# The last product of VectorE's exponentials on GpSimd, narrower products of P, and three smaller edits

## The chip, the core and the metric

The kernel runs on one core of a Trainium2 chip. The core has five engines with queues of their own that wait for one another through semaphores: TensorE (PE in the profile; its weight loads are PEld), VectorE (DVE), ScalarE (ACT), GpSimd (POOL) and SyncE (SP), which here only issues transfers. The metric is the time of one execution on the device. The kernel before takes 808.6 us, the median of three runs (807.6 to 808.67).

## The reference

Two attention blocks read the same input `x` (2048 rows of 512), and a gate per row mixes their results:

```
g = sigmoid(sum(x * gate_w))                       # one number per row
A: q, k, v = x @ wqkv_A   (32 heads of 16)
   P = softmax(q k^T / 4);  a = (P v) @ wo_A       # 32 x 2048 x 2048 exponentials
B: q, k, v = x @ wqkv_B
   phi(t) = where(t > 0, t + 1, exp(t)) + 1e-6
   b = (phi(q) (phi(k)^T v) / (phi(q) sum phi(k))) @ wo_B
out = g * a + (1 - g) * b
```

The work lies in A: a score and an exponential for each head, query and key, and the product of the exponentials with v. B is linear in the rows and small.

## The kernel before

**Units and rounds.** A unit is 128 keys by 512 queries of one head. A round is four heads and 512 queries, that is 64 units; there are 32 rounds and 2048 units. The score matmul of a unit uses 32 of TensorE's 128 rows, and three such matmuls of different heads run side by side. They write three PSUM banks: banks 0 to 2 and 3 to 5 are two slots that take turns (`SLOTS`). ScalarE then makes the exponentials of a whole slot with one instruction (L1540), 1536 columns wide into the buffer `PT`.

**The second source of exponentials.** For some units VectorE makes the exponential. The unit is claimed in one of two ways. It takes the third bank of a slot, so that ScalarE's instruction is only 1024 wide (`claim_in_group`), or it takes the spare bank (`claim_beside`, `misc_step`). VectorE copies the score from PSUM into `YI` as a clamped 16-bit integer (L1186). Three claimed units make a triple of 1536 columns, and `close_tri` queues five instructions for it, all from SBUF to SBUF in `DP`: g from the bits of y (L1200), h from the low bits of y (L1202), w = h * h (L1204), e from the high bits of g (L1205), and w = w * g (L1207). The exponential is a weighted sum of e, g and w; the weights are in two scaled copies of v, `V2`. So a unit from VectorE enters TensorE as three stationary operands where one from ScalarE enters as one.

**Products of P.** `pv_fns` multiplies 128 queries of a unit (stationary) with v (moving). A moving operand is 64 columns: 32 of `Vaug` (16 of v, a column of ones for the row sum, zeros) and 32 columns of zeros beside them. All products of a round gather in one bank, `acc_bank`; after 64 units `round_end` divides by the row sum, multiplies with the gate and sends the result by a transposing transfer to `OT`.

**Everything else** runs between these: the projections for A's next 128 columns of q, k and v, all of B, the gate (`step_gate`), and the output matmuls. Each such step takes one spare bank (`MISC`, bank 7), in pieces of two to sixteen matmuls, where `misc_step` finds room.

**What sets the order.** The program is laid out in advance by a planner in the kernel's Python code. It keeps an estimated clock for each engine (`PE.t`, `AC.t`, `DV.t`), with constants for each kind of work: `QK_T`, `PV_T` (four products of P), `d_sb` and `d_psum` for VectorE, `LAT` for a wait. The main loop (to L1575) issues a slot's scores, then ScalarE's instruction. Until the next slot is free by that clock it fills TensorE with products of P, steps and claims. `pump` hands queued VectorE work out by priority; the triples have the lowest. On the chip the engines follow the order so made, each in its own queue; a semaphore wait that the planner took to be short can be long. `mac_share` adds up how much of TensorE's array the last 3 us used, and where it is under `MAC_LOW` (0.5), `fill` adds a matmul of zeros (`warm`). GpSimd has only the preparations of the first 13 us.

**The start.** The first slots are woven with the transposes and projections that they need (`stage`, `run_now`), each in a bank from `rot_bank`, which from the first slot on has bank 7 alone. **The end.** Four output blocks are left: two are copied by ScalarE (L1616), two get their first part added by VectorE (L1621), all into `outl`, which lies in the `g` part of `DP`. Each of the four names all of `r_G` as written, so each waits for the one before.

## Time and profile before

| | |
|---|---|
| median of three runs | 808.6 us |
| the profiled execution: time, span | 809.02 us, 807.3 us |
| ScalarE busy | 788.0 us (98% of the span); L1540 x649 |
| TensorE busy | 768.8 us (95%); products of P x10976 |
| VectorE busy | 734.9 us (91%); 348 units, 116 triples |
| GpSimd busy | 11.5 us (1%) |
| first and last L1540 | starts at 9.0 us, ends at 799.1 us |

Busy time counts a stretch once even when two instructions of an engine overlap in it. On ScalarE and VectorE the next instruction starts before the one before has ended, so what an instruction costs its engine is the time from its start to the next start, shorter than its own duration. TensorE's ends are modelled, so there too start to start is the measure. The row of granted clock says what part of TensorE's full clock was granted.

### The profile page before, as it was taken

How to read it: one execution, taken by the hardware profiler on the slowest of the kernel's cores; microseconds unless marked ns; L12 is line 12 of the kernel's file. 1: busy time of each engine (PE TensorE's matmuls, PEld its weight loads, DVE VectorE, ACT ScalarE, POOL GpSimd, SP SyncE). 2: the span in 40 equal slices, each digit the busy share in tenths (PEclk: the TensorE clock that was granted, in tenths of full speed). 3: DMA queues.
4: the chain of work that ended last, by engine and by line, in shares of the span. 5: the costliest groups of instructions: out<-in, count | busy, mean ns of one | idle time of the engine just before them, and what ended most of it. 6: DMA issues, size and time to landing. Idle time of an engine off the chain costs nothing.

```text
span 807.3 us, 31603 instructions
## 1 busy us (share of the span) xinstructions
PE 768.8 (95%) x14060; PEld 478.4 (59%) x14060; DVE 734.9 (91%) x1253; ACT 788.0 (98%) x689; POOL 11.5 (1%) x21
## 2 busy tenths in 40 slices
PE   7999999999999999999999999999999999999997
PEld 3655655655565666555556566556665556565664
DVE  4689999798999999998999999999999998999983
ACT  5899999999999999999999999999999999999996
POOL 5000000000000000000000000000000000000000
PEclk9889999999999999999999999999999999999999
DMA  9200000000000001000000100101111001000100
GB/s 252 86 9 15 2 2 16 2 14 4 2 15 3 15 4 9 9 2 15 2 16 9 22 16 9 28 9 16 29 22 29 9 19 25 10 22 15 22 3 30
DMA packets 32492, 16.96 MB, mean 21 GB/s; under 512 B 24608, under 2 KB 31200, under 8 KB 32352
## 3 DMA queue, kind: packets, MB, share of 16 engines
q1 hardware_dynamic: 30336, 13.32, 7.0%
q8 instruction: 112, 1.84, 0.9%
q10 hardware_dynamic: 2016, 1.57, 0.8%
q14 instruction: 28, 0.23, 0.1%
HBM read 5.90 MB, written 2.10 MB: 10 GB/s over the span
## 4 chain that ended last, share of the span: by engine, by line
PE 40%; ACT 39%; issue 14%; DVE 7%; ACTq 0%; POOL 0%; DVEq 0%; POOLq 0%
PE ps L525 39%; ACT PT L1540 38%; DVE YI L1186 1%; ACT epool L791 1%; DVE DP L1204 1%; DVE DP L1207 1%; DVE DP L1200 0%; PE ps L528 0%; DVE xT L1457 0%; DVE DP L1205 0%; DVE DP L1202 0%; DVE phi L796 0%; DVE Vaug L745 0%; DVE Osb L1049 0%; DVE KT L690 0%
## 5 line engine op out<-in xcount | busy, mean ns | idle before, releaser
L1540 ACT ACTIVATE PT<-ps 128x1536 bf16<-128x1536 f32 (+1 forms) x649 | 780.6, 1558 | 6.8 <-PE ps L525 6.6
L525 PE MATMUL ps<-Qpad,KT 32*128 32x512 bf16 x2048 | 272.9, 387 | 25.3 <-ACT PT L1540 15.7
L525 PEld LDWEIGHTS ps<-Vaug,PT 128*128 128x128 bf16 x6800 | 230.1, 98 | 110.9 <-issue 105.9
L525 PE MATMUL ps<-Vaug,PT 128*128 128x64 bf16 x6800 | 287.9, 195 | 0.3 <-DVE Osb L1049 0.2
L1186 DVE TENSOR_SCALAR YI<-ps 128x512 int16<-128x512 f32 x348 | 239.3, 688 | 23.4 <-PE ps L525 13.2
L525 PE MATMUL ps<-Vaug,DP 128*128 128x64 bf16 x4176 | 163.1, 194 | 1.2 <-DVE Osb L1049 1.2
L525 PEld LDWEIGHTS ps<-Vaug,DP 128*128 128x128 bf16 x4176 | 138.4, 98 | 25.5 <-issue 18.2
L525 PEld LDWEIGHTS ps<-Qpad,KT 32*128 32x128 bf16 x2048 | 69.0, 91 | 138.8 <-ACT PT L1540 106.0
L1204 DVE TENSOR_TENSOR DP<-DP 128x1536 bf16<-128x1536 uint16 x116 | 110.8, 955 | 2.5
L1207 DVE TENSOR_TENSOR DP<-DP 128x1536 bf16<-128x1536 bf16 x116 | 110.3, 951 | 0.0
L1200 DVE TENSOR_SCALAR DP<-YI 128x1536 uint16<-128x1536 uint16 x116 | 64.3, 554 | 0.9
L1202 DVE TENSOR_SCALAR DP<-YI 128x1536 uint16<-128x1536 uint16 x116 | 64.2, 553 | 0.0
L1205 DVE TENSOR_SCALAR DP<-DP 128x1536 uint16<-128x1536 uint16 x116 | 63.9, 551 | 0.0
L525 PE MATMUL ps<-wB,xT 128*128 128x512 bf16 x128 | 37.6, 382 | 1.3 <-DVE phi L796 1.1
L525 PE MATMUL ps<-xT,wA 128*128 128x512 bf16 x108 | 31.9, 391 | 0.0
L791 ACT ACTIVATE epool<-ps 128x512 bf16<-128x512 f32 x32 | 27.7, 866 | 0.0
L796 DVE SCALAR_TENSOR_TENSOR phi<-ps,epool 128x512 bf16<-128x512 f32 x32 | 22.0, 688 | 1.6
L525 PE MATMUL ps<-xT,wB 128*128 128x512 bf16 x64 | 18.3, 381 | 0.0
L525 PE MATMUL ps<-woA,OT 128*128 128x512 bf16 x64 | 18.0, 381 | 0.0
L745 DVE CAST Vaug<-ps 128x512 bf16<-128x512 f32 x16 | 11.0, 689 | 7.6 <-PE ps L525 7.3
L525 PE MATMUL ps<-woB,OBT 128*128 128x512 bf16 x64 | 17.5, 381 | 0.1
L1047 DVE RECIPROCAL rraw<-ps 128x16 f32<-128x16 f32 x32 | 8.1, 253 | 9.1 <-PE ps L525 9.0
(85 smaller groups left out, 244.4 us busy)
## 6 DMA issues: line engine op xcount, KB each, us to landing
Qpad<-Qs SPq DMA_DIRECT2D x124, 16.0 KB, 1.8
wA<-in_A_wqkv_dram SPq DMA_DIRECT2D x1, 1536.0 KB, 7.0
wB<-in_B_wqkv_dram SPq DMA_DIRECT2D x1, 1536.0 KB, 10.6
out_dram<-outt SPq DMA_DIRECT2D x12, 128.0 KB, 1.7
phi<-in_A_x_dram ACTq DMA_DIRECT2D x3, 256.0 KB, 6.1
PT<-in_A_x_dram ACTq DMA_DIRECT2D x1, 512.0 KB, 3.9
woA<-in_A_wo_dram SPq DMA_DIRECT2D x1, 512.0 KB, 12.1
woB<-in_B_wo_dram SPq DMA_DIRECT2D x1, 512.0 KB, 11.9
```

Of the source, the lines that this page charges most:

```text
L525: return lambda: nc.tensor.matmul(o, lhsT=l, rhs=r, start=start, stop=stop, skip_group_check=sg)
L745: ops = [(lambda: nc.vector.tensor_copy(Vaug[:, par, 4 * v:4 * v + 4, :, 0:16], src), [r_bank[b]], [r_V[par][v]], d_psum(512), lambda: v_d ...
L791: op(AC, lambda: nc.scalar.activation(epool[:, s, :], bank_ap(b), ACT.Exp), reads=[r_bank[b]], writes=[r_e[s]], dur=0.6, issue=0.48)
L796: (lambda: nc.vector.scalar_tensor_tensor(out=dst, in0=bank_ap(b), scalar=0.0, in1=epool[:, s, :], op0=ALU.max, op1=ALU.add), [r_bank[b], ...
L1047: (lambda: nc.vector.reciprocal(raw, acc4[:, :, :, 16]), [r_acc], [r_rraw], 0.26, None),
L1186: push(0 if in_group else 1, [(lambda: nc.vector.tensor_scalar(YI[:, yi, 512 * k:512 * (k + 1)], bank_ap(b), Y_LO, Y_HI, op0=ALU.max, op1= ...
L1200: (lambda: nc.vector.tensor_scalar(gb, y, 0x8000, 3, op0=ALU.bitwise_xor, op1=ALU.logical_shift_right), [r_YI[yi]], [r_G[dp]], d_sb(n, 0.2 ...
L1202: (lambda: nc.vector.tensor_scalar(hh, y, 0x3FF, 0x400, op0=ALU.bitwise_and, op1=ALU.bitwise_or), [r_YI[yi]], [r_DP[dp]], d_sb(n, 0.25), N ...
L1204: (lambda: nc.vector.tensor_tensor(w, hh, hh, ALU.mult), [r_DP[dp]], [r_DP[dp]], d_sb(n, 0.5), None),
L1205: (lambda: nc.vector.tensor_single_scalar(eb, gb, 0xFF80, ALU.bitwise_and), [r_G[dp]], [r_E[dp]], d_sb(n, 0.25), None),
L1207: (lambda: nc.vector.tensor_tensor(w, w, g, ALU.mult), [r_DP[dp], r_G[dp]], [r_DP[dp]], d_sb(n, 0.5), None)])
L1540: op(AC, lambda slot=slot, b0=b0, n=n: nc.scalar.activation(PT[:, slot, 0:n], ps[:, 512 * b0:512 * b0 + n], ACT.Exp, scale=LN2 / FRAC, bia ...
```

## The change

- **Last product.** `w = w * g` leaves VectorE's queue and is issued on GpSimd as soon as the planner has issued `w = h * h`. Products of P from `DP` now wait for GpSimd. The planner takes `0.3 us + n * 2.2 ns` for it, that is 3.68 us for 1536.
- **52 columns.** The moving operand of a product of P is 26 columns of v and 26 of zeros in place of 32 and 32. The planner's `PV_T` goes from 0.117 to 0.1012.
- **Gate.** Its matmuls come in 16 pieces of four in place of four of sixteen, and a piece is put off while `mac_share` is under 0.4.
- **Start.** Until the first product of P, `rot_bank` also uses the accumulator's bank; the first v projection goes behind the fourth slot in place of the first.
- **End.** The four output copies no longer name `r_G`.
- **Planner's numbers.** `PT_URGENT`, `PV_LAG`, `LATE`, `MIN_LEFT`, `CLAIM_LOAD` and `GPR` are set anew, so the whole order differs. The plan that comes out has 393 units and 131 triples on VectorE and 361 + 286 instructions L1540 of 1536 and 1024 columns, where before it had 348 units, 116 triples and 403 + 245 (and one of 512). The matmuls of zeros go from 27 to 45 (13 of them in the start in both).

```diff
-PV_T = 0.117
+PVW = 26
+PV_T = 0.1012
+PV_MAC = 0.087
+POOL_FIX, POOL_T = 0.3, 2.2e-3
...
+        GATE_N = 1
+        GATE_MAC = .4
...
-                for t in range(NQC):
+                for t in range(0, NTB, GATE_N):
                     fns = []
-                    for tb in range(4 * t, 4 * t + 4):
+                    for tb in range(t, t + GATE_N):
...
-                    out_.append((fns, rd, 0.6, 0.01))
+                    out_.append((fns, rd, 0.15 * GATE_N, 0.0025 * GATE_N))
...
-                if c + 64 <= 512:
-                    mv = bass.AP(tensor=v0.tensor, offset=own, ap=[list(v0.ap[0]), [zero_off - own, 2], [1, 32]])
-                    o = acc[:, c:c + 64]
+                if c + 2 * PVW <= 512:
+                    mv = bass.AP(tensor=v0.tensor, offset=own, ap=[list(v0.ap[0]), [zero_off - own, 2], [1, PVW]])
+                    o = acc[:, c:c + 2 * PVW]
...
-        PT_URGENT = 15
+        PT_URGENT = 13
...
-                     dur=PV_T * n, mac=0.107 * n)
+                     dur=PV_T * n, mac=PV_MAC * n)
...
-        MIN_LEFT, MIN_LEFT_LAST = 30, 24
+        MIN_LEFT, MIN_LEFT_LAST = 24, 24
...
+            def last_product():
+                op(PO, lambda: nc.gpsimd.tensor_tensor(w, w, g, ALU.mult), reads=[r_DP[dp], r_G[dp]], writes=[r_DP[dp]],
+                   dur=POOL_FIX + n * POOL_T)
...
-                (lambda: nc.vector.tensor_tensor(w, hh, hh, ALU.mult), [r_DP[dp]], [r_DP[dp]], d_sb(n, 0.5), None),
+                (lambda: nc.vector.tensor_tensor(w, hh, hh, ALU.mult), [r_DP[dp]], [r_DP[dp]], d_sb(n, 0.5), last_product),
                 (lambda: nc.vector.tensor_single_scalar(eb, gb, 0xFF80, ALU.bitwise_and),
-                 [r_G[dp]], [r_E[dp]], d_sb(n, 0.25), None),
-                (lambda: nc.vector.tensor_tensor(w, w, g, ALU.mult), [r_DP[dp], r_G[dp]], [r_DP[dp]], d_sb(n, 0.5), None)])
+                 [r_G[dp]], [r_E[dp]], d_sb(n, 0.25), None)])
...
-        GPR = 16.9
+        GPR = 16.6
...
+                if hold[0][2][0][3] < 0.01 and mac_share(now) < GATE_MAC:
+                    return False
...
-        CLAIM_LOAD = 4.0
+        CLAIM_LOAD = 5.0
...
-        PV_LAG = 15
-        LATE = 12
+        PV_LAG = 13
+        LATE = 14
...
-        V0_AT = 1
+        V0_AT = 4
...
-            b = misc_banks[bank_turn[0] % len(misc_banks)]
+            banks = misc_banks + [acc_bank[0]] if acc_n[0] == 0 and acc_round[0] == 0 else misc_banks
+            b = banks[bank_turn[0] % len(banks)]
...
-            op(AC, lambda k=k, o=o: nc.scalar.copy(outl[:, k, :], o), reads=[r_bank[free[k]]], writes=[r_outl[k]] + r_G, dur=0.6)
+            op(AC, lambda k=k, o=o: nc.scalar.copy(outl[:, k, :], o), reads=[r_bank[free[k]]], writes=[r_outl[k]], dur=0.6)
...
-               reads=[r_bank[free[k]], r_pre[k]], writes=[r_outl[k]] + r_G, dur=d_psum(512))
+               reads=[r_bank[free[k]], r_pre[k]], writes=[r_outl[k]], dur=d_psum(512))
```

More of the change, by code (lines that the diff above doesn't have):

```diff
@@ L1012, in pv_fns @@
                 c = 128 * qb + 32 * j
-                if c + 64 <= 512:
-                    mv = bass.AP(tensor=v0.tensor, offset=own, ap=[list(v0.ap[0]), [zero_off - own, 2], [1, 32]])
-                    o = acc[:, c:c + 64]
-                else:
-                    mv = bass.AP(tensor=v0.tensor, offset=zero_off, ap=[list(v0.ap[0]), [own - zero_off, 2], [1, 32]])
-                    o = acc[:, c - 32:c + 32]
+                if c + 2 * PVW <= 512:
+                    mv = bass.AP(tensor=v0.tensor, offset=own, ap=[list(v0.ap[0]), [zero_off - own, 2], [1, PVW]])
+                    o = acc[:, c:c + 2 * PVW]
+                else:
+                    mv = bass.AP(tensor=v0.tensor, offset=zero_off, ap=[list(v0.ap[0]), [own - zero_off, 2], [1, PVW]])
+                    o = acc[:, c - PVW:c + PVW]
                 fns.append(f_mm(o, p_ap[:, 128 * qb:128 * (qb + 1)], mv, start=(first and qb == 0), stop=False, sg=True))
```

## The prediction

> **What bounds the kernel now.** First the page's busy times, then the stretches by stage: from 65 to 760 us ScalarE is hardly ever idle, while TensorE and VectorE are each idle a few per cent.

> ```profile
> PE 768.8 (95%) x14060; PEld 478.4 (59%) x14060; DVE 734.9 (91%) x1253; ACT 788.0 (98%) x689; POOL 11.5 (1%) x21
> ...
> PE 40%; ACT 39%; issue 14%; DVE 7%; ACTq 0%; POOL 0%; DVEq 0%; POOLq 0%
> ```
> ```profile
> 30.00:35.00 5.00, 4.98 (x131) 3.75 (x126) 4.72 (x9) 4.33 (x5) 0.00 (x0) 1.00 0.02 3
> 35.00:45.30 10.30, 9.94 (x109) 5.39 (x109) 7.54 (x15) 7.97 (x9) 0.00 (x0) 0.50 0.01 2
> ...
> 200.00:400.00 200.00, 192.90 (x3600) 120.53 (x3596) 189.67 (x327) 200.00 (x181) 0.00 (x0) 1.00 0.04 8
> ```

> Columns: stretch, length, busy time of PE, PEld, DVE, ACT, POOL, granted clock, DMA share, GB/s. ScalarE sets the pace, and from 35 to 45.3 us TensorE ran at half clock and left ScalarE idle for 2.3 us. What an exponential costs ScalarE is read start to start:

> ```profile
> L1540 ACT ACTIVATE PT<-ps 128x1536 bf16<-128x1536 f32 x403 | 592.0, 1715 | 3.7 <-PE ps L525 3.6
> L1540 ACT ACTIVATE PT<-ps 128x1024 bf16<-128x1024 f32 x245 | 272.6, 1301 | 3.1 <-PE ps L525 3.0
> ```

> From start to start, with nothing to wait for, the trace has 1.330 us behind a 1536 and 0.903 behind a 1024, though each itself lasts longer; behind an epool (B's exponential) it is 0.477. The sum 403 x 1.330 + 245 x 0.903 + 0.5 + 32 x 0.477 + 0.1 is 773.1 us of the 790.1 from the first L1540 (9.0) to the end of the last (799.1). So only 17 us are lost there: 2.9 before 20 us, 5.0 from 20 to 60, and about 0.24 per 20 us after. Faster means fewer ScalarE columns, if TensorE and VectorE can carry what ScalarE drops.

> **The change, part by part.**

> *ScalarE.* The changed program's order has 361 of 1536 and 286 of 1024, no 512, and the same 32 epool. Its sum is 361 x 1.330 + 286 x 0.903 + 15.3 + 0.1 = 753.8: **19.3 us less**. The 41 more short ones cost something, because behind a 1024 TensorE has less time to refill the slot: the mean start-to-start loss is 0.05 us behind a 1024 and 0.02 behind a 1536, so 41 x 0.05 = **+2**.

> *VectorE.* From start to start the trace gives: L1186 0.60, L1200, L1202 and L1205 0.47 (0.57 where the next waits for it), L1204 and L1207 0.87 each:

> ```profile
> 302.13 0.55 DVE L1205 TENSOR_SCALAR DP<-DP 128x1536 uint16<-128x1536 uint16 x1
> 302.60 0.95 DVE L1207 TENSOR_TENSOR DP<-DP 128x1536 bf16<-128x1536 bf16 x1
> 303.47 0.56 DVE L1200 TENSOR_SCALAR DP<-YI 128x1536 uint16<-128x1536 uint16 x1
> ```

> Removed: 116 x 0.87 = 101 us. Added: 15 triples of 3 x 0.60 + 0.47 + 0.57 + 0.87 + 0.47 = 4.18, 63 us. All VectorE work start to start is 714 before, so 676 after: 86% of a shorter span where it was 88%. It hides under ScalarE as before, if nothing slows it.

> *GpSimd.* 131 products of 1536 columns, two inputs and one output, all in SBUF. No row shows one. Nearest rows: filling 8192 columns took 6.92 us (0.84 ns a column, one write); a select (one read, one write) took 0.19 us at 8 columns and 0.29 and 0.34 at 128, so 0.8 to 1.2 ns a column over a fixed 0.19. If a second read adds one such pass, the product is 0.2 + 1536 x (1.7 to 2.4 ns) = 2.8 to 3.9 us; I take 3.3, the middle. [...] 131 x 3.3 is 432 us of 785, so GpSimd is not the bound; the planner counts 3.68, so up to there products of P from `DP` come no earlier than their data. At 3.9 TensorE would wait up to 0.2 us per triple, 29 us if all were bare; nearly all of it can hide while TensorE has slack. Cost taken: 0, bounds 0 and 29.

> *TensorE.* A 64-column product of P, and what a narrow matmul costs at least:

> ```profile
> 28.88 0.52 PE L525 MATMUL ps<-Vaug,PT 128*128 128x64 bf16 x12
> 29.66 1.57 PE L525 MATMUL ps<-Vaug,PT 128*128 128x64 bf16 x48
> ...
> 32.27 0.55 PE L525 MATMUL ps<-gw,xT 128*128 128x1 bf16 x16
> 33.07 0.95 PE L525 MATMUL ps<-gw,xT 128*128 128x1 bf16 x32
> ```

> (1.57 - 0.52) / 36 = 29 ns for 64 columns; (0.95 - 0.55) / 16 = 25 ns for one column. 52 columns lie between: by proportion 24, so the 25 binds. 10976 x 29 = 318 us become 11336 x 25 = 283, while 18 more matmuls of zeros at 0.217 add 4: TensorE gets 31 us lighter. It is not the bound, so this buys no time itself; it keeps TensorE from becoming the bound when ScalarE quickens. Were 52 columns as dear as 64, TensorE would instead grow by 10 + 4 us while the span shrinks by 24; its busy share would pass ScalarE's in places (a rival).

> *Clock.* The gate's 64 one-column matmuls stand at 32.3 to 34.0 and 38.9 us; in the 3.4 us from 32 the array's use was 0.22, and at 35.05 the granted clock halved, for 10.2 us. In steady state the use falls to 0.39 at the least and the clock stays whole. Between 35 and 46 us ScalarE lost 3.1 us. The changed order puts at most 12 gate matmuls together, with products of P between. **-3.1**; bounds -3.1, and +3 for one such stretch elsewhere, since narrower products lower the use (mean 0.66) by some 0.05.

> *Start.* The losses up to 35 us other than the clock's are 2.9 plus 1.7 (0.52 at 21, 0.35 at 27, 0.78 at 30); the largest, 1.4 at 13.7, is TensorE waiting for VectorE's copies out of the one spare bank. A second bank overlaps these, but a later first v heaps up products of P, as in the x48 run above. Bounds -4.6 and +1.5; I take the middle, **-1.5**.

> *End.*

> ```profile
> 801.86 0.58 ACT L1616 CAST DP<-ps 128x512 bf16<-128x512 f32 x1 [2.71 <-PE ps L525]
> ...
> 802.89 0.58 ACT L1616 CAST DP<-ps 128x512 bf16<-128x512 f32 x1 [0.45 <-PE ps L525]
> ```
> ```profile
> 803.58 0.69 DVE L1621 TENSOR_TENSOR DP<-ps,phi 128x512 bf16<-128x512 f32 x1 [2.07 <-ACT DP L1616]
> ...
> 804.38 0.68 DVE L1621 TENSOR_TENSOR DP<-ps,phi 128x512 bf16<-128x512 f32 x1
> ```

> VectorE waited 2.07 us for ScalarE's copy only through `r_G`. Its block is TensorE's second of four, so its first add can start near 802.1 and the second end near 803.6 in place of 805.06. Then ScalarE's own second store (issued at 803.51) is next to last. **-1.4**; bounds 0 and -1.6.

> Sum against the profiled execution: 809.02 - 19.3 + 2 - 3.1 - 1.5 - 1.4 = **785.7**, taken as 786. That execution is 0.4 above the median; both stand within what a measurement of this kernel tells from no change, 0.2% or 1.6 us.

> **The rivals.**

> *1. GpSimd's product shuts VectorE out.* L1200, L1202, L1205 (0.30 ns a column) and L1204 (two SBUF operands) go through SBUF alone; the other 1.8 us of a triple, L1186, comes from PSUM. If GpSimd's product and such an instruction exclude each other for their whole length, VectorE stands still whenever one comes up too early. In the changed order, between a product and the next such instruction (L1205 let past) there is PSUM work of 1.34 us on average, and none at 28 of 131. The sum of what is missing to 3.3 us is 260 us. VectorE's 676 becomes 936, plus some 20 at the ends: **956 us**; 896 at 2.8 us, 1032 at 3.9. The chain: claimed units stay in their banks, TensorE's scores wait for these, ScalarE for the scores. It decides once the mean stall passes 786 - 20 - 676 = 90 us over 131, 0.7 us a product. The trace is nearly silent: GpSimd's last instruction ends at 12.7 us and the first triple comes some 20 us later. Beside GpSimd's 6.92 us fill, three VectorE fills of 256 columns in SBUF started at once and took 0.27 us each: both can be in SBUF together, at least where neither reads and VectorE goes at 0.83 ns a column. [...] Chance 0.20: the only side-by-side rows speak against an exclusion of every kind, but none has a quick instruction.

> *2. They only slow each other.* GpSimd is busy 3.3 of 5.9 us per triple; of the 2.37 us of SBUF work 1.3 falls beside it. A slowing by half to double costs 0.65 to 1.3 us a triple, 85 to 170 us against 90 of slack: **786 to 866**, middle 815. Chance 0.09.

> *3. TensorE eats the gain:* the product comes later than 3.68, or 52 columns cost 29 ns. Of 29 to 45 us (33 + 12) of added TensorE time about a third shows, since its idle share is some 8%: **797**. For it: the planner's order fixes every wait beforehand. Against: the one-column row. Chance 0.09.

> **How the numbers follow.** The forecast, 776 to 796 around **786**, gets 0.62: losses along the way by bounds of +-5, start and clock together +-5. Rivals 1 to 3 have 0.20, 0.09, 0.09. Faster by over 0.2%: 0.62 + 0.08 of rival 3 = 0.70; within: 0.03 (edge of 2 and 3); slower: 0.20 + the rest, 0.27. The range leaves rival 1 out whole: **775 to 820**.

> **What would show it.** Right: start-to-start 1.33 and 0.90 on ScalarE unchanged, its busy share still 98%, products of P at 25 ns, no row of half clock at 35 us, GpSimd near 3.3 us each, L1621 without a wait for ScalarE. Wrong by rival 1: L1200, L1202 or L1204 with idle time released by GpSimd or with durations of several us, and L1540 waiting for scores. By rival 2: the same rows at 0.7 to 1 us in place of 0.55. By rival 3: weight loads of `Vaug,DP` waiting for GpSimd.

## The result and the profile after

The changed kernel takes 1038.4 us (median; 1034.5 to 1039.0) where the kernel before, beside it, takes 808.6: a ratio of 1.283, 95% interval 1.280 to 1.286. The forecast of 786 us and its range of 775 to 820 were wrong; the first rival, that GpSimd's product shuts VectorE out, names what happened. It had a chance of 0.20, and its 956 us were 82 too low.

The page's busy times and its chain of the changed kernel (profiled execution: 1034.5 us, span 1032.7):

```profile
PE 817.4 (79%) x14330; PEld 496.3 (48%) x14438; DVE 941.6 (91%) x1242; ACT 797.4 (77%) x687; POOL 427.3 (41%) x152
...
DVE 57%; PE 27%; issue 13%; ACT 1%; DMA 1%; POOL 0%; POOLq 0%; SPq 0%; DVEq 0%; ACTq 0%
```

ScalarE's share falls from 98% to 77% and it leaves the chain (39% before, 1% now); VectorE goes from 7% of the chain to 57%. The groups show which of its instructions grew (form, count, busy time in us and mean duration in ns, idle time before them). First before:

```profile
L1186 DVE TENSOR_SCALAR YI<-ps 128x512 int16<-128x512 f32 x348 | 239.3, 688 | 23.4 <-PE ps L525 13.2
L1200 DVE TENSOR_SCALAR DP<-YI 128x1536 uint16<-128x1536 uint16 x116 | 64.3, 554 | 0.9
L1205 DVE TENSOR_SCALAR DP<-DP 128x1536 uint16<-128x1536 uint16 x116 | 63.9, 551 | 0.0
L794 DVE TENSOR_SCALAR epool<-epool 128x512 bf16<-128x512 bf16 x32 | 9.2, 289 | 2.5 <-ACT epool L791 2.2
L1048 DVE TENSOR_TENSOR rden<-rraw,gom 128x16 f32<-128x16 f32 x32 | 5.6, 175 | 1.1
```

Then the changed kernel:

```profile
L1193 DVE TENSOR_SCALAR YI<-ps 128x512 int16<-128x512 f32 x393 | 269.3, 686 | 44.8 <-PE ps L529 30.5
L1215 DVE TENSOR_SCALAR DP<-DP 128x1536 uint16<-128x1536 uint16 x131 | 191.2, 1459 | 0.0
L1214 DVE TENSOR_TENSOR DP<-DP 128x1536 bf16<-128x1536 uint16 x131 | 124.8, 953 | 1.9
L1210 DVE TENSOR_SCALAR DP<-YI 128x1536 uint16<-128x1536 uint16 x131 | 107.9, 824 | 1.0
L1212 DVE TENSOR_SCALAR DP<-YI 128x1536 uint16<-128x1536 uint16 x131 | 99.9, 763 | 0.0
L801 DVE TENSOR_SCALAR epool<-epool 128x512 bf16<-128x512 bf16 x32 | 48.7, 1522 | 1.1 <-ACT epool L798 1.1
L1055 DVE TENSOR_TENSOR rden<-rraw,gom 128x16 f32<-128x16 f32 x32 | 23.5, 735 | 0.9
```

(In the changed kernel L1193 is the PSUM copy that was L1186; L1210, L1212, L1214 and L1215 are g, h, w = h * h and e; L801 and L1055 were L794 and L1048.) The copies from PSUM kept their 0.69 us. Of the instructions from SBUF to SBUF, w = h * h kept its 0.95 (none of its 131 started beside a product); e went from 0.55 to 1.46 us, g to 0.82, h to 0.76, epool's from 0.29 to 1.52, the 16-column rden from 0.18 to 0.74. The excess is 131 x (0.91 + 0.27 + 0.21) + 32 x (1.24 + 0.56) = 240 us, and half of it, 119 us, is e's. It does not appear as idle time: an instruction that is shut out counts as running. The timeline around one product shows what they wait for, GpSimd first, then VectorE (start, duration):

```profile
400.63 3.09 POOL L1207 TENSOR_TENSOR DP<-DP 128x1536 bf16<-128x1536 bf16 x1 [3.73 <-DVE DP L1214]
```
```profile
400.47 2.28 DVE L1193 TENSOR_SCALAR YI<-ps 128x512 int16<-128x512 f32 x3
402.67 1.47 DVE L1215 TENSOR_SCALAR DP<-DP 128x1536 uint16<-128x1536 uint16 x1
404.06 0.55 DVE L1210 TENSOR_SCALAR DP<-YI 128x1536 uint16<-128x1536 uint16 x1
```

Three PSUM copies run beside the product. L1215 starts at 402.67, inside it, and ends at 404.14, 0.42 us after the product's end at 403.72. The trace has 65 of these L1215 that started inside a product. One started 0.08 us before the product's end and took its usual 0.55; the other 64 ended 0.414 to 0.422 us after the product did, whether they lasted 0.79 or 3.34 us. That is a wait until GpSimd has finished, not a slowing.

TensorE and ScalarE show the consequence. Ahead of its score matmuls TensorE was idle for 25.3 us in the kernel before. In the changed kernel it is 121.5 us, most of it until VectorE has copied a score and so freed its bank. ScalarE in turn waits for the scores, 115 and 101 us where it was 3.6 and 3.0:

```profile
L529 PE MATMUL ps<-Qpad,KT 32*128 32x512 bf16 x2048 | 306.2, 430 | 121.5 <-DVE YI L1193 67.9 <-DVE phi L803 15.6 <-DVE Osb L1056 11.7
L1553 ACT ACTIVATE PT<-ps 128x1536 bf16<-128x1536 f32 x361 | 511.2, 1464 | 118.6 <-PE ps L529 115.4
L1553 ACT ACTIVATE PT<-ps 128x1024 bf16<-128x1024 f32 x286 | 287.0, 1042 | 102.9 <-PE ps L529 101.4
```

A stretch of 200 us (columns as in the prediction):

```profile
200.00:400.00 200.00, 157.17 (x2822) 95.96 (x2840) 185.71 (x246) 153.84 (x136) 82.91 (x27) 0.86 0.03 6
```

Where ScalarE was busy 200.0 of these 200 us before, it is busy 153.8, and the granted clock is 0.86: TensorE, busy 157 us where it was 193, ran at half clock (0.50) for 277 us of the whole execution.

### The profile page after: what moved, and what is told of

Read it like the earlier page. It is cut to its first block, busy times and chain, and to the rows that moved or that the text cites. A ratio compares the mean times of both kernels' runs of the same rounds, so it can differ in the third digit from the quotient of the medians.

```text
span 1032.7 us, 32544 instructions
## 1 busy us (share of the span) xinstructions
PE 817.4 (79%) x14330; PEld 496.3 (48%) x14438; DVE 941.6 (91%) x1242; ACT 797.4 (77%) x687; POOL 427.3 (41%) x152
## 3 DMA queue, kind: packets, MB, share of 16 engines
q10 hardware_dynamic: 2016, 1.57, 0.6%
## 4 chain that ended last, share of the span: by engine, by line
DVE 57%; PE 27%; issue 13%; ACT 1%; DMA 1%; POOL 0%; POOLq 0%; SPq 0%; DVEq 0%; ACTq 0%
PE ps L529 27%; DVE YI L1193 14%; DVE DP L1215 10%; DVE DP L1210 7%; DVE DP L1214 6%; DVE DP L1212 6%; DVE epool L801 3%; DVE rden L1055 2%; DVE phi L803 2%; DVE Osb L1056 1%; ACT PT L1553 1%; DVE KT L694 1%; DVE Qs L726 1%; DVE OB L903 1%; DVE Vaug L749 1%
## 5 line engine op out<-in xcount | busy, mean ns | idle before, releaser
L1207 POOL TENSOR_TENSOR DP<-DP 128x1536 bf16<-128x1536 bf16 x131 | 415.8, 3174 | 594.5 <-DVE DP L1214 594.5
L529 PE MATMUL ps<-Qpad,KT 32*128 32x512 bf16 x2048 | 306.2, 430 | 121.5 <-DVE YI L1193 67.9
L1193 DVE TENSOR_SCALAR YI<-ps 128x512 int16<-128x512 f32 x393 | 269.3, 686 | 44.8 <-PE ps L529 30.5
L529 PE MATMUL ps<-Vaug,PT 128*128 128x52 bf16 x6620 | 271.2, 192 | 7.2 <-DVE outt L963 2.6
L1215 DVE TENSOR_SCALAR DP<-DP 128x1536 uint16<-128x1536 uint16 x131 | 191.2, 1459 | 0.0
L529 PE MATMUL ps<-Vaug,DP 128*128 128x52 bf16 x4716 | 186.5, 194 | 5.6 <-DVE phi L803 2.4
L529 PEld LDWEIGHTS ps<-Vaug,DP 128*128 128x128 bf16 x4716 | 160.6, 102 | 45.4 <-issue 34.9
L1214 DVE TENSOR_TENSOR DP<-DP 128x1536 bf16<-128x1536 uint16 x131 | 124.8, 953 | 1.9
L1210 DVE TENSOR_SCALAR DP<-YI 128x1536 uint16<-128x1536 uint16 x131 | 107.9, 824 | 1.0
L1212 DVE TENSOR_SCALAR DP<-YI 128x1536 uint16<-128x1536 uint16 x131 | 99.9, 763 | 0.0
L801 DVE TENSOR_SCALAR epool<-epool 128x512 bf16<-128x512 bf16 x32 | 48.7, 1522 | 1.1 <-ACT epool L798 1.1
L1055 DVE TENSOR_TENSOR rden<-rraw,gom 128x16 f32<-128x16 f32 x32 | 23.5, 735 | 0.9
```

The lines of the kernel that those rows point to most:

```text
L529: return lambda: nc.tensor.matmul(o, lhsT=l, rhs=r, start=start, stop=stop, skip_group_check=sg)
L801: (lambda: nc.vector.tensor_scalar(epool[:, s, :], epool[:, s, :], 1.0, 1e-6, op0=ALU.min, op1=ALU.add), [r_e[s]], [r_e[s]], 0.29, None),
L1055: (lambda: nc.vector.tensor_tensor(rv, raw, gv, ALU.mult), [r_rraw, r_g], [r_rden[k]], 0.18, None),
L1193: push(0 if in_group else 1, [(lambda: nc.vector.tensor_scalar(YI[:, yi, 512 * k:512 * (k + 1)], bank_ap(b), Y_LO, Y_HI, op0=ALU.max, op1= ...
L1207: op(PO, lambda: nc.gpsimd.tensor_tensor(w, w, g, ALU.mult), reads=[r_DP[dp], r_G[dp]], writes=[r_DP[dp]], dur=POOL_FIX + n * POOL_T)
L1210: (lambda: nc.vector.tensor_scalar(gb, y, 0x8000, 3, op0=ALU.bitwise_xor, op1=ALU.logical_shift_right), [r_YI[yi]], [r_G[dp]], d_sb(n, 0.2 ...
```

## The experiments

Three explanations fit the result. **Exclusion:** GpSimd's product shuts VectorE's quick instructions out. **Clock:** the narrower products of P lower the use of TensorE's array until the clock halves, and the rest follows. **Lateness:** the product is ready later than the planner thinks and TensorE waits for it.

**e1: the product back on VectorE.** All else stays as changed.

```diff
...
-                (lambda: nc.vector.tensor_tensor(w, hh, hh, ALU.mult), [r_DP[dp]], [r_DP[dp]], d_sb(n, 0.5), last_product),
+                (lambda: nc.vector.tensor_tensor(w, hh, hh, ALU.mult), [r_DP[dp]], [r_DP[dp]], d_sb(n, 0.5), None),
...
-                 [r_G[dp]], [r_E[dp]], d_sb(n, 0.25), None)])
+                 [r_G[dp]], [r_E[dp]], d_sb(n, 0.25), None),
+                (lambda: nc.vector.tensor_tensor(w, w, g, ALU.mult), [r_DP[dp], r_G[dp]], [r_DP[dp]], d_sb(n, 0.5), None)])
```

> The changed kernel with the last product of a triple back in VectorE's queue; the four other parts and the planner's numbers as changed. Its order has 405 + 237 exponentials of 1536 and 1024 columns (and one of 512), 119 triples and 91 matmuls of zeros. Theory (GpSimd's product shuts VectorE's quick SBUF instructions out for its whole length): nothing of it is left, VectorE's rows are those of before, no half clock in steady state. By the sum on record: ScalarE 4.6 us less than before, gate -3.1, start -1.5, end -1.4, so 798 us, 792 to 806. Rival (the narrower products of P lower the array's use so far that the clock halves by itself): the half-clock stretches stay and the time stays above 900. Rival (the product only comes late and TensorE waits): also some 798, it does not tell these two apart.

803.3 us (800.3 to 812.0; ratio to before 0.9947, interval 0.9918 to 0.9977). The product on GpSimd is the whole loss; the four other parts and the new planner's numbers together gain a little. The spread is wider than before's (807.0 to 809.6) and goes with the granted clock: 800.3 us at 0.998, 812.0 at 0.977. In its profiled run, of 811.4 us, TensorE ran at half clock in four stretches, 37.5 us in all, the longest from 28 to 49 us:

```profile
28.30:48.80 20.50, 20.05 (x319) 13.05 (x320) 14.01 (x26) 15.86 (x14) 0.00 (x0) 0.50 0.01 2
48.80:195.00 146.20, 137.62 (x2629) 82.01 (x2626) 140.51 (x238) 145.45 (x130) 0.00 (x0) 1.00 0.04 9
```

So the half clock is worth some 10 us here (812.0 us at 0.977 against 800.3 at 0.998), not 230; e7 and e6 below ask what brings it.

**e2: the product on GpSimd alone**, in the kernel before, with its 64 columns, gate, start, end and numbers: e1's diff the other way round, on the other kernel.

> The kernel before with nothing changed but the last product on GpSimd: 64 columns, the old gate, start, end and numbers; 118 triples. Theory (exclusion): the quick instructions that meet a product last until it ends; some 1.8 us lost per product as in the changed kernel, so 118 x 1.8 = 212 us on 800: about 1010, 960 to 1050. Rival (narrow products cause the half clock): close to 800, since 64 columns hold the clock.

1004.9 us, one run. 118 products cost 197 us over before, 1.7 each, and e (L1210 here) is long again:

```profile
L1210 DVE TENSOR_SCALAR DP<-DP 128x1536 uint16<-128x1536 uint16 x118 | 161.1, 1365 | 0.0
```

With 64 columns the loss is there too: the clock explanation falls as the main cause. The granted clock is 0.889 here, although 64 columns held it at 0.99 or more in every run of the kernel before. So most of the half clock of the changed kernel comes with the waiting, and not from the narrow products.

**e3: a product nobody waits for.** e1's kernel; GpSimd multiplies two weight tiles in 20 of 32 rounds.

```diff
+            def beside():
+                if act_round[0] >= 20:
+                    return
+                oo = outt[:].rearrange("p a n -> p (a n)")
+                for _ in range(1):
+                    deps = _deps_for([r_DP[dp], r_woA, r_woB], r_outt + r_wA0)
+                    _record(PO, PO.add(lambda: nc.gpsimd.tensor_tensor(oo[:, 0:n], woA[:].rearrange("p a n -> p (a n)")[:, 0:n], woB[:].rearrange("p a n -> p (a n)")[:, 0:n], ALU.mult), deps), [], r_outt + r_wA0)
...
-                (lambda: nc.vector.tensor_tensor(w, hh, hh, ALU.mult), [r_DP[dp]], [r_DP[dp]], d_sb(n, 0.5), None),
+                (lambda: nc.vector.tensor_tensor(w, hh, hh, ALU.mult), [r_DP[dp]], [r_DP[dp]], d_sb(n, 0.5), beside),
```

> As e1, the real product on VectorE, but in the first 20 of 32 rounds GpSimd also multiplies two weight tiles into a tile that is free then, 1536 columns, started by the same w = h * h; nobody waits for it. Theory (exclusion): some 75 products cost 1.8 us each although none is needed: e1 + 135, about 930; L1200 to L1207 are long in the first two thirds and as in e1 in the last. Rival (TensorE waits for a late product): no different from e1.

941.2 us, one run: 138 over e1 for 73 products, 1.9 each, where 135 were expected. Lateness falls: nothing reads the result, and the trace has no wait for these products. The trace has its own control, a stretch with products and one with only the last of them:

```profile
200.00:400.00 200.00, 162.00 (x2675) 92.14 (x2672) 187.39 (x248) 155.64 (x137) 75.00 (x24) 0.85 0.03 6
640.00:790.00 150.00, 138.81 (x2682) 83.01 (x2683) 145.78 (x247) 148.99 (x128) 3.08 (x1) 1.00 0.11 20
```

Once GpSimd stops, ScalarE is busy 149.0 of 150 us and the clock is whole. VectorE's instructions with two SBUF inputs are shut out as well, even the smallest. GpSimd, then VectorE:

```profile
262.62 3.09 POOL L1213 TENSOR_TENSOR outt<-woA,woB 128x1536 bf16<-128x1536 bf16 x1 [5.89 <-DVE DP L1219]
```
```profile
263.06 0.24 DVE L1054 RECIPROCAL rraw<-ps 128x16 f32<-128x16 f32 x1
263.34 2.40 DVE L1055 TENSOR_TENSOR rden<-rraw,gom 128x16 f32<-128x16 f32 x1
265.77 0.42 DVE L1056 TENSOR_TENSOR Osb<-ps,rden 128x256 bf16<-128x256 f32 x1
```

L1055 multiplies 16 columns, 0.18 us of work, and takes 2.40, to 0.03 us after the product's end at 265.71. It is part of a round's division, for which the accumulator's bank waits.

**e4: two fills in place of e3's product.**

```diff
-                for _ in range(1):
+                for _ in range(2):
...
-                    _record(PO, PO.add(lambda: nc.gpsimd.tensor_tensor(oo[:, 0:n], woA[:].rearrange("p a n -> p (a n)")[:, 0:n], woB[:].rearrange("p a n -> p (a n)")[:, 0:n], ALU.mult), deps), [], r_outt + r_wA0)
+                    _record(PO, PO.add(lambda: nc.gpsimd.memset(oo[:, 0:n], 0.0), deps), [], r_outt + r_wA0)
```

> As e3 with two fills of 1536 columns (about 1.35 us each) by GpSimd in place of the product: it writes and reads nothing. If GpSimd's instructions exclude VectorE's whatever they do: 75 x 2.7 us of occupied time, some 75 x 1.3 = 100 us lost, about 900. If only what reads does: as e1, under 810. If it depends on the kind of VectorE instruction (those with two inputs against those with one, written twice as fast), the rows of L1204 and L1207 stay at 0.95 and those of L1200, L1202 and L1205 grow, or the other way round.

837.0 us, one run: 34 over e1 for nearly the same GpSimd time (73 x 2 fills of 1.49 us against 73 products of 3.15). So it is neither all nor nothing, it depends on the kind of VectorE instruction, the third case of the expectation. GpSimd's two fills, then VectorE:

```profile
61.64 3.11 POOL L1213 MEMSET outt<- 128x1536 bf16 x2 [3.33 <-DVE DP L1219]
```
```profile
62.70 0.73 DVE L1220 TENSOR_SCALAR DP<-DP 128x1536 uint16<-128x1536 uint16 x1
63.35 0.67 DVE L1193 TENSOR_SCALAR YI<-ps 128x512 int16<-128x512 f32 x1
63.95 0.94 DVE L1222 TENSOR_TENSOR DP<-DP 128x1536 bf16<-128x1536 bf16 x1
```

L1222, w = w * g with two SBUF inputs, starts inside the second fill and takes its usual 0.94. All 43 that started inside a fill took 0.94 to 0.95; all 10 that started inside a product of e3 were long, 2.3 to 3.9 us. L1220 (e), one input and 0.30 ns a column, waits for the first fill (0.73 here, up to 1.57). So in these traces L1222, with two SBUF inputs, waits beside a GpSimd instruction that reads SBUF and not beside one that only writes, with 10 rows on one side and 43 on the other.

**e10: a third of e3's product**, 512 columns, on e6 (below).

```diff
-                    _record(PO, PO.add(lambda: nc.gpsimd.tensor_tensor(oo[:, 0:n], woA[:].rearrange("p a n -> p (a n)")[:, 0:n], woB[:].rearrange("p a n -> p (a n)")[:, 0:n], ALU.mult), deps), [], r_outt + r_wA0)
+                    _record(PO, PO.add(lambda: nc.gpsimd.tensor_tensor(oo[:, 0:512], woA[:].rearrange("p a n -> p (a n)")[:, 0:512], woB[:].rearrange("p a n -> p (a n)")[:, 0:512], ALU.mult), deps), [], r_outt + r_wA0)
```

> As e6 with e3's idle product in the first 20 rounds, but 512 columns wide, which should last about 1.2 us. If the loss is what is missing between the product's end and the PSUM work that stands behind it in VectorE's order: summed over the 73 products 23 us at 1.2 us, where the same sum at 3.15 us gives 145 and e3 measured 138 over e1. So 815 to 830. If each GpSimd instruction costs a fixed time: as e3, 138 more, about 938. If the loss goes with the time that GpSimd is busy: 138 x 1.2 / 3.15 = 53, about 853.

816.7 us, one run: 17 over e6. The product lasted 1.21 us:

```profile
L1213 POOL TENSOR_TENSOR outt<-woA,woB 128x512 bf16<-128x512 bf16 x73 | 88.4, 1211 | 416.2 <-DVE DP L1219 416.2
```

A third of the width costs an eighth, as expected if what counts is what is left of the product when the PSUM work behind it is done (815 to 830). A loss per instruction (138) or in proportion (53) is ruled out.

**e9: a delay without GpSimd**, on e6: VectorE fills 1536 columns that nobody needs behind each w = h * h in the first 20 rounds.

```diff
...
+                _record(DV, DV.add(lambda: nc.vector.memset(oo, 0.0), deps), [], r_outt + r_wA0)
...
```

> As e6, but in the first 20 of 32 rounds VectorE also fills 1536 columns that nobody needs right behind each w = h * h: 73 fills of about 0.71 us, 52 us that the planner does not know of; GpSimd does nothing. It asks whether VectorE's idle time is a reserve, as the forecast's rival took it (time passes 786 only once the stall is over 90 us in all). VectorE has some 50 us idle in e6, two thirds of it in these rounds. If it is a reserve: at most + 20, 820 or less. If in a fixed order a stall of VectorE is passed on nearly whole: + 45 to 55, 845 to 855.

847.2 us, one run: 47 over e6, for

```profile
L1212 DVE MEMSET outt<- 128x768 uint32 x73 | 51.0, 698 | 8.0
```

51 us of work. VectorE's idle time is no reserve: it is 57 us in e9 and 51 in e6, so the delay used none of it, and some nine tenths of a delay that the planner does not know are passed on. A few of the 47 us may be the half clock's (granted clock 0.985, 0.998 in e6); a reserve would have left at most 20.

**e5: an order that knows the exclusion.** The changed kernel with one more resource in the planner, `r_port`, which g, h, e, h * h, epool's and rden's instruction read and the product writes, and e formed ahead of w = h * h.

```diff
-        r_eg, r_g = R("eg"), R("g")
+        r_eg, r_g, r_port = R("eg"), R("g"), R("port")
...
-                op(PO, lambda: nc.gpsimd.tensor_tensor(w, w, g, ALU.mult), reads=[r_DP[dp], r_G[dp]], writes=[r_DP[dp]],
-                   dur=POOL_FIX + n * POOL_T)
+                _emit(PO, lambda: nc.gpsimd.tensor_tensor(w, w, g, ALU.mult), [r_DP[dp], r_G[dp]], [r_DP[dp], r_port],
+                      POOL_FIX + n * POOL_T)
```

> The changed kernel with a planner that knows the exclusion: VectorE's quick instructions (those from SBUF to SBUF, also the two small ones of epool and rden) are planned behind a running product and PSUM copies are put beside it, and e is formed ahead of w = h * h, so that nothing quick of the same triple is left. It then claims 98 triples; ScalarE has 455 + 194 exponentials (and one of 512), by start to start 796 us against 754 in the changed kernel. Theory (exclusion): the long rows go, most of the loss with them; 796 + 9 + 8 at the ends + 15 = about 830, 820 to 860, which is still slower than before: known in advance, the exclusion costs claims in place of stalls. Rival (what costs is GpSimd's product or its semaphores as such): 98 x 1.9 = 186 us stay, about 985.

830.4 us, one run, as expected. No row is long any more; e's, for one:

```profile
L1214 DVE TENSOR_SCALAR DP<-DP 128x1536 uint16<-128x1536 uint16 x98 | 54.1, 552 | 0.0
```

and the clock is 0.996. But only 98 triples find room, fewer than the 116 of the kernel before, so ScalarE has more to do. In this plan, handing the product to GpSimd does not pay even with the exclusion known; its other numbers were not tuned for it.

**e7 and e6: the half clock of e1.** e7 is e1 with 64 columns and their planner's numbers; e6 is e1 with more matmuls of zeros:

```diff
-PVW = 26
-PV_T = 0.1012
-PV_MAC = 0.087
+PVW = 32
+PV_T = 0.117
+PV_MAC = 0.107
```
```diff
-        MAC_LOW = 0.5
-        MAC_END, END_FROM = 0.55, 44
+        MAC_LOW = 0.7
+        MAC_END, END_FROM = 0.7, 44
```

> As e1 with 64 columns in products of P and the planner's old numbers for them. The plan then leaves ScalarE 387 + 269 exponentials (and one of 512), 773.4 us start to start, 4.9 more than e1's 768.5. If narrow products bring the half clock: no spread, clock 0.99 or more, about 805 in every run; 52 columns are worth 5 us while the clock holds. If the gate, the start or chance bring it: spread as in e1.

> As e1 with matmuls of zeros put in where the array's use over 3 us is under 0.7 in place of 0.5 (0.55 at a round's end): 203 in place of 91, all where the planner sees TensorE free; ScalarE's and VectorE's counts are those of e1. e1 spread from 800.3 us at a granted clock of 0.998 to 812.0 at 0.977. If the spread is the half clock that the narrow products bring, it goes: 800 to 802 in every run, clock over 0.995. If it is something else, the spread stays, and the zeros cost up to 112 x 0.22 = 24 us.

e7: 805.2 us (805.1 to 806.2; ratio 0.9964, interval 0.9952 to 0.9977), clock 0.999, no spread. e6: 799.9 us (799.0 to 800.5; ratio 0.9894, interval 0.9874 to 0.9913), no spread. The use of TensorE's array over the steady state (columns times rows, over the time at full clock) is 0.66 on average in e7 and in the kernel before, 0.61 in e1 and 0.65 in e6; apart from the last 3 us, the profiled runs have 37.5 us at half clock in e1, none in e7 and 3.4 in e6. So, without the product on GpSimd, the half clock comes with the narrow products and all but goes when zeros fill the array where TensorE has time; 112 more of them cost nothing that can be seen. **e6 beats both kernels**, the one before by 1%. ScalarE is again without a gap:

```profile
200.00:400.00 200.00, 192.60 (x3630) 113.65 (x3627) 193.94 (x339) 200.00 (x181) 0.00 (x0) 1.00 0.04 8
```

**e8: the end alone**, in the kernel before, and **e11: e6 with the old start.**

```diff
-            ... writes=[r_outl[k]] + r_G, ...
+            ... writes=[r_outl[k]], ...
```
```diff
-        V0_AT = 4
+        V0_AT = 1
...
-            banks = misc_banks + [acc_bank[0]] if acc_n[0] == 0 and acc_round[0] == 0 else misc_banks
+            banks = misc_banks
```

> The kernel before with the four output copies no longer naming the g part: everything else in the same order. The sum on record has -1.4 us, bounds 0 and -1.6: 807.0 against 808.4. L1621 no longer waits for ScalarE.

> As e6 with the start of before: v of the first rounds behind the first slot, one spare bank in the start. ScalarE's and VectorE's counts and the zeros are those of e6. The sum on record had -1.5 us for the new start, bounds -4.6 and +1.5: so 801.4, 798.4 to 804.5, against e6's 799.9. e6's profile loses 2.5 us of ScalarE's time before 60 us where before lost 7.9, 3.1 of it to the half clock; if all of the other 2.3 is the start, 802.2.

e8: 807.7 against 807.9 us, ratio 0.9991, interval 0.9978 to 1.0005: not told from no change. Its trace has the mechanism, no wait for ScalarE, and 5.2 us from the copy L1600 to the span's end in place of 6.4:

```profile
802.71 0.69 DVE L1621 TENSOR_TENSOR DP<-ps,phi 128x512 bf16<-128x512 f32 x1 [0.57 <-PE ps L525]
```

e11: 804.5 us (801.3 to 806.5; ratio 0.9947, interval 0.9925 to 0.9969) against e6's 799.9; with the new start the kernel is 4 to 5 us faster. Most of it goes with the half clock, since e11's spread is back, and its profile has a stretch from 36.3 to 46.5 us. At equal granted clock little is left: e11's two runs at 0.998 and 0.999 took 801.3 us each, e6's four, all at 0.998, took 799.0 to 800.5. That leaves some 1.4 us for the start itself, an estimate from two runs.

## Why the prediction was wrong

**The step that failed** is VectorE's: "It hides under ScalarE as before, if nothing slows it." Something did. GpSimd's product held off VectorE's e, g, h, epool's and rden's instruction until it had ended: the 121 of these that started inside a product of the changed kernel ended 0.03 to 0.47 us after it. The long rows of the changed kernel add up to 1.83 us per triple; e1 takes the product away and with it the loss, and e3 brings 1.9 per product back with a product that nobody needs. The condition had been seen, as rival 1, with the right mechanism and 1.98 us a product. That it came so near is in part luck: the rival let L1205 (e) past, and e took half of the stall, 0.91 us per triple, while L1204, which it named, never met a product.

**Its chance was set by a row that could not tell.** Three VectorE fills of 256 columns beside GpSimd's fill were taken as evidence against. By e3 and e4 the kind decides on both sides (beside GpSimd's fills e took up to 1.57 us and w = w * g its 0.94 to 0.95; beside its products w = w * g took 2.3 to 3.9): those VectorE fills read nothing and go at 0.83 ns a column, and GpSimd's fill reads nothing. The row lacked both features that the rival needed, and the prediction said so, yet leaned on it. No row of the kernel before has a product on GpSimd beside a quick VectorE instruction, so the 0.20 was the author's estimate.

**Its price, 956 us, was too low** because 90 us of VectorE's idle time were counted as a reserve. By e9 47 of 51 us are passed on: the order is fixed, and a late VectorE makes TensorE and then ScalarE late, while the idle time lies elsewhere. With no reserve, 786 + 240 us of excess in the long rows gives 1026, within 1% of the 1034.5 of the profiled execution. The other runs agree: the excess of their long rows is 191 us in e2 (197 over before), 121 in e3 (138 over e1), 35 in e4 (34 over e1) and 19 in e10 (17 over e6). What the 277 us at half clock add was not separated; if the excess is passed on whole, these sums leave some 10 to 20 us for it.

**The other terms.**

- ScalarE, -19.3: the costs held (1.33 and 0.90 us start to start where nothing is waited for), but the counts behind it came from a plan that VectorE could not keep. With the product back on VectorE the plan gives 4.6.
- GpSimd's product, 3.3 us: 3.17 on average, 3.09 where nothing disturbs it. Not too late for TensorE, whose weight loads waited 2.6 us for it in all; rival 3 did not occur. Its second half did not either: products of P at 52 columns stand 25 ns apart, as worked out.
- TensorE, no time of its own: right as far as it goes. Through the planner 52 columns gain about 5 us (e7 against e6, which also has more zeros).
- Clock, -3.1: wrong for this kernel. With 64 columns, the gate in pieces and the new start, the stretch at 35 us is gone (e7: 0.999 or more in all seven runs). With 52 columns it is not sure to be: e1 has stretches at half clock in the start and in steady state, by chance, and with the old start e11 has one at 36 us in spite of the pieces. The bound of +3 allowed for one such stretch; e1's profiled run has four and takes 811.4 us, where the fastest takes 800.3. The stretch in the kernel before was itself worth about 2 us, since its runs at a clock of 1.0 took 807.0 to 807.2.
- Start, -1.5 within -4.6 and +1.5: some -1.4 at equal clock (e11 against e6), -4 to -5 with the clock's share.
- End, -1.4: 1.1 by the traces, below what the runs can tell.

Without the product, the sum on record gave 798; e1 measures 803.3, and e6, whose zeros keep the clock, 799.9.

## What to carry to other kernels

Before work moves to GpSimd beside a busy VectorE, list VectorE's instructions by their operands: in these traces those that go quickly from SBUF to SBUF (one input, 0.30 ns a column) and those with two SBUF inputs wait out a GpSimd product, whole (121 starts inside one in the changed kernel, all with their end 0.03 to 0.47 us after its end), while copies from PSUM do not (85 of them started inside a product of the changed kernel and took 0.68 to 0.69 us). A profile shows this as long durations and not as idle time. In an order fixed in advance, do not count an engine's idle share as a reserve: price an unplanned stall at its full length, as e9 and the long rows have it here. When matmuls are narrowed, look at the granted clock of several runs, and compare the spread as well as the median.
